# A gated mix of two long convolutions: four PSUM copies merged in pairs, and a hand-written order permuted

## The chip, the cores and the metric

The kernel runs on one core of one Trainium2 chip. The metric is device time in microseconds of one execution, as the median over several executions. The core's engines are named as the profile names them: PE (matrix multiply, with its weight loads shown as PEld), DVE (vector), ACT (scalar and activation functions), POOL (which here makes index tables and starts DMAs) and SP (which only starts DMAs). Each runs its own list of instructions in order; semaphores tie the lists together.

## The reference

Two sequence mixers work on the same input `x` of 2048 positions by 448 channels, and a gate of one value per position mixes their results. Each mixer is a causal convolution as long as the sequence, written as an FFT product. In A the convolution kernel `K` is itself computed, from 256 complex modes per channel; in B it is given.

```python
# A: u = x
dt = exp(log_dt)[:, None]; A = A_re + 1j*A_im; dB = dt*(B_re + 1j*B_im)
P = exp((dt*A)[:, :, None] * arange(2048))           # 448 x 256 x 2048
K = einsum("dn,dnl,dn->dl", C_re + 1j*C_im, P, dB).real
a = irfft(rfft(u, 4096) * rfft(K, 4096))[:2048] + u*Dskip
# B: q = x
k_shift = sum over t of k_pad[t : t+2048] * shift_k[:, 3-t]   # 4 taps
kv = k_shift * v
b = q * (irfft(rfft(kv, 4096) * rfft(ssm_k, 4096))[:2048] + kv*ssm_D)
# out
g = sigmoid((x * gate_w).sum(-1))
out = g*a + (1-g)*b
```

Inputs and output are bfloat16.

## The kernel before

**Work and tiling.** The 448 channels are cut into four groups `H` of 112 (28 columns in each of four partition blocks). For each group the kernel does three kinds of work, listed in `PLAN`: a table `T` (the sine and exponential tables of A's modes, their products, and from them K), a convolution of mixer B (`B`, `b`), and one of mixer A (`a`, for the last group `A`). For groups 0 to 2 a step `m` (`mix`, from line 1071) adds the two results and turns them to the output's layout; for the last group `end` (from line 980) does this in four quarters, `h` and `k` from 0 to 1.

A convolution is a Fourier transform written as matrix products in two levels: `spread` and `transform` go forward; `swapped` makes a copy with real and imaginary halves exchanged, by eight small DMAs; `products` multiplies the two spectra on DVE, two operations of 128 x 3584; `stage_a` and `stage_b` come back. After each block of matrix products the result is copied from PSUM to SBUF.

**Who copies.** The class `Sides` (line 346) gives each of some 400 such small steps to DVE or to ACT by one letter of the string `SIDES`: V is DVE, S is ACT. The same string decides for each of `swapped`'s DMAs whether POOL's queue (V) or SP's (S) starts it. Lines 355 to 390 hold the kinds of step: plain copy, add, scale and add, mask, negate.

**Order.** The program's 6,393 calls are not issued where they are written. `Order` (line 133) records them in a list, and `issue` (line 140) issues them in the order of the string `ORDER`, a permutation written out in runs of numbers. Each instruction is tied behind the one before it on its engine, so `ORDER` fixes every engine's list, DMA queues included. `SLOTS` and `ROOMS` (read in `slot` and `room`, lines 161 to 168) say which of eight SBUF buffers `q0` to `q7` and which of four PSUM rooms `ps0` to `ps3` each step uses. A room is two PSUM banks wide.

All instructions are issued from one line, so the profile shows L145 for all of them, and one tells them apart by tile and shape.

**Modes.** `Modes.run` (line 718) makes what the tables start from. For `A_re` and `A_im` it takes one room, with 448 values in each of its two banks (bank `f`), and copies it into three buffers: one holds group 0 (`hold`), one group 1, one groups 2 and 3. Every buffer is filled by two copies, one for each bank, so there are 2 x 3 x 2 = 12 copies. The groups' log-steps then feed `exps` and `levels`, which scale 224 columns at a time for the exponential and the sine.

**The start.** ACT's first step is to load the table of functions for the exponential; it then takes the exponential of `log_dt`, which a DMA brings. Sines need the other table, so ACT loads tables five times in the program.

**The end.** In `end`, each quarter does 33 matrix products (the sum over `G`), then on DVE a multiplication by the gate and an addition (`RK`), then 16 short matrix products (`relay`), then a negating copy (`q<-ps` 128x448), then four DMAs to the output, two on SP's queue and two on ACT's:

```python
evac.minus(laid(line(y0)[:, 0:4], H), pt[:, 0:448].rearrange(...))
for x in range(4):
    dmae[x % 2].dma_start(out_rows[x][:, y0:y0 + 4], lines[h][...])
```

In the built program the DMAs of SP and ACT take eight completion counters in turn, and a DMA that takes a counter again first waits, on the engine that starts it, until the earlier DMA of that counter has landed.

Of the kernel before, what the change touches and what calls it, by code (L numbers as in the profile page):

```python
# [24 lines left out]
NC = 112 // NQG  # L25
# [13 lines left out]
    "60254113451327565066707216435622473722641555230367571061240"  # L39
)  # L40
ROOMS = (
    "303201320132221133023000100332000020101102013331223132233010132231223133020313021221212111021000320232120101311331120231"
    "31230230312202203230211002013123100022133320222302200321202302202333012331301212103331312131332201202032310"
)
SIDES = (
    "SSSSVVSVVVVSVVSVVVVVVVVVSVVVSSVVVSSSSSVSVVSSVVSVVSVSSVVSVVVVVVVSSSSSSSSSSSSSSSSSVVVSVSSSVSSSSSSSSSSSSSSSSVSSSSVSVSSSSSSS"
    "SSSSSSSSSSSSSVSSVSSSSSSSSSSVSSSSSSSSSSSSSSSSSSVVSVSSSSSSSSSSSSSSSSSVVVVVVVVVSVVSVVVSSSSSSVSSSSSSSSSSSSVVSVSSSSSSSSSSVSVV"
    "SSSSSSSSSSSVSSSVVSSSSSSSSSSSVSSSSVVVVVVVVSVVVVSVVVSSSVSVVSSSSSSSSSSVVVSVVSSSSSSSSSSSSSSVSSSSSVSSSSSSVSSVSVSSVSSSSVSVVSSS"
    "VSSSSVSSVVVVSSSSSSSSSSVVVSSSSVSSSSVSSSVVSS"
)  # L50
ORDER = (
# [650 lines left out]
class Modes:  # L702
# [15 lines left out]
    def run(self):  # L718
        nc, V, evac = self.nc, self.nc.vector, self.evac
        for c, nm in enumerate(("A_re", "A_im")):  # L720
            pt = self.stepped(nm)
            for h0, h1, t in self.hold:
                for f in range(2):
                    evac(t[:, :, c].rearrange("p h (q w) -> p q h w", w=NC)[:, 4 * f:4 * f + 4],
                         pt[:, f, 0:448].rearrange("p (g h w) -> p g h w", g=4, w=NC)[:, :, h0:h1])
# [401 lines left out]
```

## Time and profile before

| | us |
|---|---|
| median of three executions | 249.13 (248.91 to 250.43) |
| the profiled execution, own time | 247.59 |
| its span, first to last instruction | 245.7 |
| granted TensorE clock, mean | 0.984 |

The profile gives for each engine the time in which it was busy, the idle time before an instruction together with what ended it, and groups of instructions of one shape with their mean duration. Durations of neighbours on an engine overlap a little, so a sum of durations is somewhat more than the busy time. A window shows the busy time of each engine in one stretch of the span. The chain of waits follows the last instruction back to whatever released it.

### The profile page before, as it was taken

The page shows a single profiled execution, that of the slowest core. Times are in us where ns is not written, and L with a number is a line of the kernel's source. Part 1 is how long each engine was busy: PE and PEld are TensorE (multiplying, and loading weights), DVE is VectorE, ACT ScalarE, POOL GpSimd, SP SyncE. Part 2 cuts the span into 40 slices and gives each one's busy share as a digit, 9 for nine tenths or more (in the row PEclk, how much of TensorE's full clock was granted, in tenths as well). Part 3 has the DMA queues.
Part 4 walks back from the last instruction along what each step waited for, and adds up shares of the span by engine and source line. Part 5 has one row for each costly group of instructions (what it writes and reads, how often), then busy time and mean ns, then how long its engine had stood idle before and what let it go on. Part 6 is the DMA issues. An engine that isn't in the chain of part 4 may idle for free.

```text
span 245.7 us, 12199 instructions
## 1 busy us (share of the span) xinstructions
PE 209.4 (85%) x5451; PEld 185.2 (75%) x5451; DVE 231.3 (94%) x399; ACT 219.0 (89%) x335; POOL 37.5 (15%) x109
## 2 busy tenths in 40 slices
PE   1557688888989999888999977999999999999970
PEld 1445256766979899788998866889999998998850
DVE  6999999999888999999999999999999999999980
ACT  3897999989999999999999999999999998657820
POOL 8600003040000014000002320000134220300000
PEclk9999799999999999999999999999999999999996
DMA  6999599999002189300476593000248720230046
GB/s 140 311 191 147 123 190 229 188 204 167 7 5 64 39 197 205 93 4 5 78 114 122 104 226 100 7 3 5 39 80 152 187 80 5 63 95 3 3 105 197
DMA packets 43443, 26.27 MB, mean 107 GB/s; under 512 B 34144, under 2 KB 40400, under 8 KB 43392
## 3 DMA queue, kind: packets, MB, share of 16 engines
q1 hardware_dynamic: 39088, 15.98, 30.6%
q0 software_dynamic: 3456, 8.60, 17.6%
q10 hardware_dynamic: 848, 0.92, 1.3%
q8 instruction: 42, 0.69, 1.1%
q14 instruction: 9, 0.07, 0.1%
HBM read 9.78 MB, written 2.87 MB: 51 GB/s over the span
## 4 chain that ended last, share of the span: by engine, by line
DVE 34%; ACT 32%; PE 21%; issue 6%; DMA 5%; DVEq 0%; ACTq 0%
PE ps L145 21%; ACT q L145 21%; DVE TQ L145 10%; DVE TP L145 9%; DVE q L145 6%; ACT G L145 4%; DVE natv L145 3%; DMA TP<-TP 2%; ACT ET L145 2%; ACT s_W L145 1%; DMA RK<-in_A_log_dt_dram 1%; DVE RK L145 1%; ACT RK L145 1%; DMA out_dram<-q 1%; DVE ET L145 1%
## 5 line engine op out<-in xcount | busy, mean ns | idle before, releaser
L145 ACT CAST q<-ps 128x896 bf16<-128x896 f32 (+3 forms) x168 | 131.6, 909 | 6.6 <-PE ps L145 6.4
L145 PEld LDWEIGHTS <-G 128*128 128x128 bf16 (+2 forms) x1136 | 35.5, 103 | 15.0 <-issue 6.0
L145 DVE TENSOR_TENSOR TQ<-TQ,ET 128x896 bf16<-128x896 bf16 (+2 forms) x70 | 45.9, 683 | 0.1
L145 PEld LDWEIGHTS <-q 128*128 128x128 bf16 (+2 forms) x784 | 41.0, 134 | 6.3 <-issue 3.5
L145 PE MATMUL ps<-q,s_W 128*128 128x112 bf16 (+1 forms) x544 | 32.6, 210 | 4.5 <-ACT q L145 2.3
L145 PE MATMUL ps<-TP,TQ 128*32 128x32 bf16 x1792 | 32.7, 240 | 2.8 <-DVE TQ L145 1.7
L145 PE MATMUL ps<-sa_R,q 128*128 128x128 bf16 x448 | 33.0, 229 | 1.5 <-issue 1.0
L145 DVE TENSOR_TENSOR q<-q,q 128x3584 bf16<-128x3584 bf16 (+1 forms) x22 | 32.3, 1510 | 1.2 <-ACT q L145 0.9
L145 PEld LDWEIGHTS <-s_W 128*128 128x128 bf16 x544 | 27.6, 97 | 7.6 <-issue 5.5
L145 PEld LDWEIGHTS <-TQ 128*32 128x32 bf16 x1792 | 29.6, 153 | 4.9 <-DVE TQ L145 1.9
L145 DVE TENSOR_TENSOR TP<-TP,ET 128x1792 bf16<-128x1792 bf16 (+3 forms) x25 | 31.7, 1270 | 0.6 <-DMA TP<-TP 0.5
L145 ACT ACTIVATE q<-hold 128x224 bf16<-128x224 f32 (+1 forms) x77 | 28.8, 461 | 0.4 <-DVE hold L145 0.3
L145 POOL DMA_DIRECT2D TP<-TP x15 | 13.4, 958 | 102.3 <-DVE TP L145 33.5
L145 POOL DMA_DIRECT2D q<-q x27 | 15.8, 638 | 57.5 <-DVE q L145 24.4
L145 PEld LDWEIGHTS <-natu 128*64 128x64 bf16 (+1 forms) x288 | 21.0, 208 | 4.6 <-DMA natu<-in_B_k_dram 3.1
L145 PE MATMUL ps<-q,G 128*128 128x56 bf16 (+1 forms) x640 | 20.3, 182 | 0.2 <-ACT q L145 0.2
L145 ACT ACTIVATE ET<-q 128x1344 bf16<-128x1344 int16 (+1 forms) x12 | 17.2, 1456 | 1.1 <-DVE TQ L145 1.0
L145 PE MATMUL ps<-Wc,natu 128*64 128x128 bf16 x224 | 16.0, 285 | 0.2 <-ACT q L145 0.2
L145 PE MATMUL ps<-Wc,natv 128*64 128x128 bf16 x224 | 15.2, 283 | 0.4
L145 PEld LDWEIGHTS <-natv 128*64 128x64 bf16 x224 | 14.7, 212 | 1.1 <-issue 0.2
L145 DVE TENSOR_TENSOR TQ<-TQ 128x448 bf16<-128x448 bf16 (+2 forms) x35 | 15.3, 443 | 0.1
L145 PE MATMUL ps<-G 112*32 112x336 bf16 (+3 forms) x448 | 13.8, 274 | 1.3 <-DVE natv L145 1.1
(97 smaller groups left out, 289.6 us busy)
## 6 DMA issues: line engine op xcount, KB each, us to landing
q<-q SPq DMA_DIRECT2D x37, 112.0 KB, 3.7
TP<-TP POOLq DMA_DIRECT2D x9, 448.0 KB, 5.8
q<-q POOLq DMA_DIRECT2D x27, 112.0 KB, 3.9
natu<-in_B_k_dram SPq DMA_DIRECT2D x2, 896.0 KB, 7.2
natv<-in_B_v_dram SPq DMA_DIRECT2D x8, 224.0 KB, 4.7
q<-in_B_ssm_k_dram SPq DMA_DIRECT2D x16, 112.0 KB, 3.9
natu<-in_A_u_dram SPq DMA_DIRECT2D x8, 224.0 KB, 5.8
TP<-TP POOLq DMA_DIRECT2D x6, 224.0 KB, 4.0
```

What stands on the lines that cost most here:

```text
L145: ins = f(*args, **kw)
```

## The change

Two things change, one small in code and one large in data.

In `Modes.run` a buffer that holds a single group is filled by one copy that reads both banks of the room (224 columns), instead of two copies of 112. The buffer of groups 2 and 3 keeps its two copies. Twelve copies become eight, and the program has 6,389 calls.

```diff
             for h0, h1, t in self.hold:
+                src = pt[:, :, 0:448].rearrange("p f (g h w) -> p f g h w", g=4, w=NC)
+                if h1 - h0 == 1:
+                    evac(t[:, 0, c].rearrange("p (f g w) -> p f g w", f=2, w=NC), src[:, :, :, h0])
+                    continue
                 for f in range(2):
-                    evac(t[:, :, c].rearrange("p h (q w) -> p q h w", w=NC)[:, 4 * f:4 * f + 4],
-                         pt[:, f, 0:448].rearrange("p (g h w) -> p g h w", g=4, w=NC)[:, :, h0:h1])
+                    evac(t[:, :, c].rearrange("p h (q w) -> p q h w", w=NC)[:, 4 * f:4 * f + 4], src[:, f, :, h0:h1])
```

All four strings are new: `ORDER`, `SIDES`, `SLOTS`, `ROOMS`. `PLAN` and every other function are as before. Read out per engine, the two programs differ like this:

- Besides the merged copies, 30 steps go from DVE to ACT and 20 from ACT to DVE. DVE has 384 instructions instead of 399, ACT 347 instead of 335, counting its table loads.
- ACT loads tables six times instead of five: a first sine, on 64 columns, now stands ahead of the exponential of `log_dt`, with its own table load.
- Eight more of the small DMAs of `swapped` go to POOL's queue: POOL starts 50 DMAs instead of 42, SP 92 instead of 100.
- The merged copies for `A_re` and `A_im` run on ACT but for one; six of the twelve were on DVE.
- In `end`, the last three quarters' relays stand one behind the other after the last sum over `G`. Before, each relay stood between two sums, and only two stood after the last one. Twelve of the sixteen output DMAs now stand behind the last three negating copies.
- Nearly every step is moved by some places within its engine's list; the sequence of the large stages is the same.

```diff
 SIDES = (
-    "SSSSVVSVVVVSVVSSVVVVVVVVVSVVVSSVVVSSSSSVSVVSSVVSVVSVSSVVSVVVVVVVSSSSSSSSSSSSSSSSSVVVSVSSSVSSSSSSSSSSSSSSSSVSSSSVSVSSSSSSS"
...
+    "SSSSVVSVVVVSVVSSVVVVVVVVSVSSSSSSVVVSSVSSVVSVVSSSVVSSSVVVSVVSSSSSSSSSSSSSSSVSVVSVVSSSVSSVSVSSSSSSSSSSSVSSSSSSSSSSSSSSSSSS"
...
```

More of the change, by code (lines that the diff above doesn't have):

```diff
@@ L38 @@
 SLOTS = (
-    "60254113451327565066707216435622473722641555230367571061240"
+    "20403116354647120522757642301265663671204711735354460250172"
 )
 ROOMS = (
-    "303201320132221133023000100332000020101102013331223132233010132231223133020313021221212111021000320232120101311331120231"
-    "31230230312202203230211002013123100022133320222302200321202302202333012331301212103331312131332201202032310"
+    "012131000231110120223323211032233303311333021332202103210131202001330010101103330222033213220320321121111121101303200031"
+    "01021032232203032203303301000222002203212132020330103132102322310010331331023320213332130130121201010013332"
 )
 SIDES = (
[L46 to L49, printed above, removed]
+    "SSSSVVSVVVVSVVSSVVVVVVVVSVSSSSSSVVVSSVSSVVSVVSSSVVSSSVVVSVVSSSSSSSSSSSSSSSVSVVSVVSSSVSSVSVSSSSSSSSSSSVSSSSSSSSSSSSSSSSSS"
+    "SSSSSSSSSSSSSVSSSSSSSSSSSSSSSSSSSSSSSSSVSVVVVVVSSSSSSSSSSSSSSSSSVVVVVSVVVVVSVVVSSSSSSVSSSSSSSSSVVVVVVSSSSSSSSSVSVSVSSSSS"
+    "SSSSSSVVVVSVSSSSSSVSSSSSSVSSVSVVVSVVVVSVVVSVVVSSSSSSSSSSSSSSSSVSVVVSVVSSSVSSSSVSSVVSSSSSSSSSSSVSSSVSSSSSSSSSSVSVSVSSSVSS"
+    "VSSSVSSSVSSSSSSSSSVVSSSSSVSVSSSSSSVSSS"
 )
 ORDER = (
[60 rows of a table removed]
[59 rows of a table added]
 )
```

119 rows, old and new, of the table ORDER are left out of this document.

## The prediction

> **What bounds the kernel now.** I read the busy times first, then windows of the span.
>
> ```profile
> PE 209.4 (85%) x5451; PEld 185.2 (75%) x5451; DVE 231.3 (94%) x399; ACT 219.0 (89%) x335; POOL 37.5 (15%) x109
> 0.00:203.10 203.10, 174.78 (x4478) 154.77 (x4478) 196.56 (x354) 194.59 (x296) 35.42 (x105) 0.99 0.56 115
> 0.00:212.00 212.00, 183.36 (x4770) 162.79 (x4771) 205.43 (x359) 201.31 (x307) 35.42 (x105) 0.99 0.54 110
> 212.00:237.50 25.50, 25.21 (x653) 21.93 (x650) 24.22 (x38) 17.10 (x28) 2.05 (x4) 1.00 0.17 44
> ```
>
> The first row is from the page. The others are windows: length, then busy time (and instructions) of PE, PEld, DVE, ACT, POOL, then granted clock and DMA share. DVE and ACT are both nearly full, and full at the same time. Up to 203.1 us ACT idles 203.1 - 194.6 = 8.5 us; up to 212.0 us DVE idles 212.0 - 205.4 = 6.6 us. So no single engine's saving comes straight off the span there: what one engine saves only counts if the other keeps up. After 212 us that is different. DVE is busy 24.2 of 25.5 us, ACT only 17.1, and PE's records fill 25.2, of which weight loads need 21.9. The tail is bound by DVE and perhaps PE, with ACT having 8 us to spare.
>
> What happens at 212 us is seen in the timeline (start, length, engine, operation, count, idle time before it):
>
> ```profile
> 208.03 3.96 DVE L145 TENSOR_TENSOR q<-q,q 128x3584 bf16<-128x3584 bf16 x2
> 236.56 0.95 PE L145 MATMUL ps<-q,G 128*128 128x28 bf16 x32
> ```
>
> The first is the last pair of wide products, for mixer A's third group; behind it come the last stages of three convolutions. The second is the last sum over G; it ends at 237.5 us, 8.2 us ahead of the span's end.
>
> **The steps that change sides.** Counted net by shape: DVE loses five mode copies, eight scalings of 224 columns or less, three negating copies of 448, one copy each of 1024 and 768 columns and one mask of 2048; it gains two copies of 512 and two of 896. ACT gains one mode copy, the eight scalings, the three negations, the 1024, the 768, the mask and a table load, and loses two 512 and two 896. What else moves cancels. The rows that price this (busy time, mean ns of one):
>
> ```profile
> L145 DVE COPY hold<-ps 128x112 f32<-128x112 f32 x3 | 0.8, 270 | 0.0
> L145 DVE TENSOR_SCALAR q<-hold 128x224 int32<-128x224 f32 x26 | 6.6, 299 | 0.0
> L145 DVE TENSOR_SCALAR q<-ps 128x448 bf16<-128x448 f32 x7 | 4.2, 618 | 0.7 <-PE ps L145 0.6 <-ACT q L145 0.2
> L145 DVE CAST q<-ps 128x512 bf16<-128x512 f32 x9 | 5.9, 685 | 0.1
> L145 DVE CAST q<-ps 128x896 bf16<-128x896 f32 x2 | 2.2, 1088 | 0.8 <-issue 0.8
> L145 DVE CAST q<-ps 128x1024 bf16<-128x1024 f32 x2 | 2.4, 1220 | 0.6 <-PE ps L145 0.6
> L145 DVE CAST q<-ps 128x768 bf16<-128x768 f32 x1 | 1.0, 953 | 0.0
> L145 DVE TENSOR_SCALAR G<-q,mask 128x2048 bf16<-128x2048 bf16 x5 | 3.6, 747 | 0.0
> L145 ACT COPY q<-ps 128x224 f32<-128x224 f32 x4 | 1.3, 336 | 1.5 <-DVE q L145 1.5
> L145 ACT ACTIVATE q<-hold 128x224 int32<-128x224 f32 x13 | 4.9, 421 | 0.0
> L145 ACT ACTIVATE q<-ps 128x448 bf16<-128x448 f32 x9 | 4.5, 546 | 5.7 <-DMA out_dram<-q 4.1 <-PE ps L145 1.6
> L145 ACT CAST q<-ps 128x512 bf16<-128x512 f32 x43 | 26.4, 637 | 3.3 <-PE ps L145 3.1
> L145 ACT COPY TQ<-ps 128x896 f32<-128x896 f32 x1 | 0.9, 897 | 0.0
> L145 ACT CAST q<-ps 128x896 bf16<-128x896 f32 x62 | 56.9, 1028 | 0.9 <-PE ps L145 0.9
> L145 ACT CAST q<-ps 128x1024 bf16<-128x1024 f32 x50 | 52.4, 1103 | 0.2 <-PE ps L145 0.2
> L145 ACT CAST q<-ps 128x768 bf16<-128x768 f32 x3 | 2.4, 812 | 1.4 <-PE ps L145 1.4
> L145 ACT ACT_TABLE_LOAD x5 | 6.4, 1283 | 1.3 <-PEq L1111 1.2
> L145 ACT ACTIVATE G<-q,mask 128x2048 bf16<-128x2048 bf16 x3 | 6.3, 2101 | 0.0
> ```
>
> The merged copy reads 224 columns from two banks; no row shows that. On ACT I take 0.34 us, the copy of the same width from one bank. On DVE it lies between one and two of the 0.27 us copies; I take 0.34 again. Six DVE copies become one: -1.62 + 0.34 = -1.28 us.
>
> *DVE:* -1.28 - 8 x 0.299 - 3 x 0.618 + 2 x 0.685 + 2 x 1.088 - 1.22 - 0.95 - 0.75 = -4.9 us of durations. *ACT:* the mode copies were four of 224 and two of 112 and become seven of 224, between 0.34 and 1.0 us more, taken as 0.5; then + 8 x 0.421 + 3 x 0.546 - 2 x 0.637 - 2 x 0.897 (the two 896 that leave are copies to TQ) + 1.10 + 0.81 + 2.10 + 1.28 = +7.7 us.
>
> Durations overlap, so fewer instructions also means fewer overlaps:
>
> ```profile
> 234.55 1.15 DVE L145 TENSOR_SCALAR q<-ps 128x448 bf16<-128x448 f32 x2
> 234.71 1.42 ACT L145 ACTIVATE q<-ps 128x448 bf16<-128x448 f32 x3 [1.35 <-PE ps L145]
> ```
>
> Two of 0.618 take 1.15 us and three of 0.546 take 1.42: about 0.09 us of overlap each on DVE, 0.11 on ACT. With 15 instructions fewer and 12 more, DVE's busy time falls by 3.5 us (4.9 if no overlap is lost) and ACT's grows by 6.4 (7.7).
>
> **Where it falls.** Walking down the new DVE list to the last wide pair, with the same prices: the merged copies (-1.28), seven scalings net (-2.09), the mask (-0.75) and a 112-wide scaling, priced like the others (-0.30), against one copy of 512 (+0.69) and three of 896 net (+3.26). That is -0.5 us with ten instructions fewer, so nothing, within 0.5 us either way. All of DVE's saving, about 4 us, lies behind the wide pair, in the tail that DVE bounds.
>
> ACT is the reverse. Up to its last copy of the transform that feeds that pair, it has +0.5 for the modes, eight scalings net (+3.4), the mask (+2.1), the table load (+1.3), three copies of 896 fewer net (-2.8), and four copies of 896 that stood behind it and are now ahead (+4.1): +8.5 us, less 1.3 for overlap, about +7. In the old order ACT's part of that transform was about done at 203.1 us, with 194.6 us of work behind it. Now it is 201.6 us of work. With the old 8.5 us of idle time it would end at 210.1, and the pair, which started at 208.0, would be 2.1 us late. So what counts is how much idle time the extra work fills. The first filler, in the timeline and the row of that sine:
>
> ```profile
> 1.20 1.28 ACT L145 ACT_TABLE_LOAD   x1 [1.20 <-PEq L1111]
> 4.22 0.21 ACT L145 ACTIVATE TP<-RK 112x4 bf16<-112x4 bf16 x1 [1.74 <-DMA RK<-in_A_log_dt_dram]
> L145 ACT ACTIVATE TP<-TP 128x64 bf16<-128x64 int16 x2 | 0.5, 264 | 0.0
> ```
>
> ACT waits 1.74 us for log_dt's DMA. The sine that moves there (0.26 us) and the second table load (1.28) go into that hole and cost the span at most 0.3 us, unless DVE makes the sine's input late; then up to 1.3. That leaves the pair 2.1 - 1.5 = 0.6 us late. Against it stands a stall that I expect to go:
>
> ```profile
> L145 DVE TENSOR_TENSOR TP<-TP,ET 128x3584 bf16<-128x3584 bf16 x9 | 18.1, 2016 | 0.5 <-DMA TP<-TP 0.5
> 129.78 5.62 DMA TP<-TP
> ```
>
> DVE waits 0.5 us for an accumulating DMA on TP, which takes 5.6 us in the chain of waits. The new order puts about 8 us of DVE work between that DMA's start and its user. I put the end of the wide pair at 212.0 us, unchanged, within 0.6.
>
> The Trainium skill, page "ScalarE: Activation LUTs", section "Table sets: the hidden batching unit", says to batch calls by table set since every switch costs a load, which speaks against the sixth load. The trace agrees on its length, 1283 ns; if it lay on the path, the forecast below would be 1.3 us higher, 249.1.
>
> **DMA queues.** The eight swaps that go to POOL stand behind POOL's accumulating DMAs, and one of the last table's accumulating DMAs now stands behind two of them, which wait for ACT's copies. From the page's list of DMA issues, and median time to landing:
>
> ```profile
> q<-q SPq DMA_DIRECT2D x37, 112.0 KB, 3.7
> q<-q POOLq DMA_DIRECT2D x27, 112.0 KB, 3.9
> ```
>
> So a moved swap lands 0.2 us later, which I count at nothing: the user of that accumulating DMA, the back half of the table, stands some 20 us of DVE work behind its source. If that cover is gone, DVE waits the difference, under 2 us.
>
> The Trainium skill, page "SBUF — State Buffer", section "SBUF: two separate sides", warns that a DMA started from POOL can be held up while DVE runs certain operations. With DVE at 94% the trace shows only those 0.2 us, so I give that rule no weight.
>
> **The tail.** DVE has 4 us less to do between 212.0 and 237.5 us. PE can give up nothing if its recorded 25.2 us is its floor, and 3.6 us if the 21.9 us of weight loads is. ACT has 8 us of room and gets about as much work as it had after the pair. I take the middle, 2.0 us: the last sum ends at 235.5.
>
> Then the output DMAs:
>
> ```profile
> 237.67 0.38 PE L145 MATMUL ps<-RK,minus 128*32 128x112 bf16 x16 [0.15 <-DVE RK L145]
> DMA to landing us min/median/max: 1.9/2.9/3.2
> 238.83 3.44 SPq L145 DMA_DIRECT2D out_dram<-q  x5
> 240.24 0.54 ACT L145 ACTIVATE q<-ps 128x448 bf16<-128x448 f32 x1 [4.12 <-DMA out_dram<-q]
> 240.81 0.86 ACTq L145 DMA_DIRECT2D out_dram<-q  x2
> 241.72 0.55 SPq L145 DMA_DIRECT2D out_dram<-q  x1
> ```
>
> The first row is a relay in the timeline, the second the output DMAs' time to landing, the others are the timeline again. The last DMA starts at 241.72, 2.9 us after the one at 238.83 whose counter it takes: it waited for that landing. From its start to the span's end are 3.9 us. In the new order three relays (0.4 us each) and ACT's two negating copies (0.54) follow the last sum, so ACT's copies are done 1.5 us behind it. ACT then starts DMAs 0.4 us apart, and the last DMA takes the counter of the second of these: started at 1.9, landed at 4.8 to 5.1, its successor started then and the span over 3.9 later, 8.8 to 9.0 us behind the last sum instead of 8.2. Without that reuse the twelve, six a queue and 0.4 apart from 1.0 on, would be out by 3.4 and the span over at 7.3. So the end costs between -0.9 and +0.8 us; I take +0.7, since the waits are in the program.
>
> **Sum.** The profiled execution took 247.59 us: span 245.7 and 1.9 outside, which stays. It becomes 247.6 + 0 - 2.0 + 0.7 = 246.3. That execution lies 1.5 us below the median of 249.13, so the forecast of the median is 249.1 - 1.3 = 247.8 us.
>
> **Rivals.** *Full gain:* PE gives up 3.6 us and the DMAs' end costs nothing: 249.1 - 3.6 = 245.5. For it: DVE's 4 us lie just where DVE is 95% busy. Against it: PE's records are full there. *ACT becomes the bound:* nothing of its other idle time is filled, the hole at the start included, so the wide pair is 2.1 us late; PE gives up nothing and the DMAs cost 0.7: 249.1 + 2.8 = 251.9. It decides from about 6.5 us of ACT idle time ahead of the pair: above that every microsecond goes to the span. For it: ACT is at 194.6 of 203.1 us already. Against it: the hole is plain. *The permutation shifts idle time only:* PE's records are its floor and the merge saves nothing that counts, so the change does not do what it says; with the DMAs, 249.1 + 0.7 = 249.8.
>
> **Numbers.** Forecast 0.43, full gain 0.25, ACT bound 0.18, shift only 0.14. The range from 245.4 to 251.2 takes in all but the ACT rival and the ends of the others. About 1% (2.5 us) is what a measurement of this kernel can tell from no change. Under 246.6 lie most of the full gain (0.22) and the low edge of the forecast (0.06): 0.28. Above 251.6 lies most of the ACT rival: 0.15. Within 1%: 0.57.
>
> **What would show it.** In the new profile: DVE busy near 227.5 us and ACT near 225; the log_dt wait on ACT nearly gone, filled by the second table load; the last 3584-wide pair ending at 212 within 0.6 (213.5 or later speaks for the ACT rival); the last sum over G ending near 235.5; ACT's busy time behind the pair above 85%; and a last output DMA that starts about 3 us behind the last copy. The forecast falls if the pair moves by more than 1.5 us either way, or if DVE idles over 3 us in the tail for PE.

## The result, and the profile after

The changed kernel takes 250.41 us (median of 20 executions, 248.86 to 252.49) against 249.24 for the kernel before beside it (20 executions). The ratio is 1.0047, 95% interval 1.0025 to 1.0068: about 1.2 us slower. Run again beside some of the experiments (e5 below) it was 1.0027 (0.9998 to 1.0055). The forecast was a gain of 1.3 us.

Its page, busy time of each engine (compare the first row of the prediction):

```profile
PE 209.8 (85%) x5451; PEld 185.1 (75%) x5451; DVE 228.2 (92%) x384; ACT 224.1 (90%) x347; POOL 42.1 (17%) x117
```

DVE lost 3.1 us and ACT gained 5.1, about as forecast. Windows, cut at the end of the last wide pair and at the end of the last sum over G:

```profile
0.00:212.08 212.08, 182.91 (x4699) 161.74 (x4701) 205.62 (x349) 201.91 (x309) 42.05 (x117) 0.96 0.57 115
212.08:238.30 26.22, 25.99 (x727) 22.81 (x723) 20.88 (x33) 21.25 (x36) 0.00 (x0) 1.00 0.03 6
```

The pair ends at 212.08 us, against 211.99 in the profile of the kernel before. Behind it the tail did not shrink: 26.2 us instead of 25.5. DVE now idles 5.3 us there, and PE is busy for 25.99 of 26.22. From the last sum to the span's end are 9.5 us instead of 8.1. So between these two profiles the loss lies behind the pair: 0.7 us in the tail and 1.3 in the end. That is more than the 1.2 us of the medians, because the profiled execution of the kernel before lies 1.5 us below its median and that of the changed kernel 0.5 below; groups of profiles further down correct for it.

The start, in the timeline of ACT: the new sine and both table loads stand where ACT waited for log_dt.

```profile
1.19 1.28 ACT L144 ACT_TABLE_LOAD   x1 [1.19 <-PEq L1113]
3.14 0.26 ACT L144 ACTIVATE TP<-TP 128x64 bf16<-128x64 int16 x1 [0.66 <-DVE TP L144]
3.41 1.28 ACT L144 ACT_TABLE_LOAD   x1
4.71 0.21 ACT L144 ACTIVATE TP<-RK 112x4 bf16<-112x4 bf16 x1
```

Around the pair, the timeline shows a wait that was not there before: ACT stands still for 4.8 us until DVE's second wide product has ended.

```profile
210.06 2.02 DVE L144 TENSOR_TENSOR q<-q,q 128x3584 bf16<-128x3584 bf16 x1
212.19 1.56 ACT L144 CAST q<-ps 128x512 bf16<-128x512 f32 x3 [4.81 <-DVE q L144]
```

The copy is the first of mixer B's last group into the buffers `pair` that two convolutions share. The new `SLOTS` puts the second half of `pair` into q6, which holds the spectrum `K` that the wide products still read. Before, it went into q7, and ACT copied from about 208 us on.

### The profile page after: what moved, and what is told of

It reads as the page before. It is cut to its first block, busy times and chain, and to the rows that moved or that the text cites. A ratio compares the mean times of both kernels' runs of the same rounds, so it can differ in the third digit from the quotient of the medians.

```text
span 247.8 us, 12203 instructions
## 1 busy us (share of the span) xinstructions
PE 209.8 (85%) x5451; PEld 185.1 (75%) x5451; DVE 228.2 (92%) x384; ACT 224.1 (90%) x347; POOL 42.1 (17%) x117
## 4 chain that ended last, share of the span: by engine, by line
ACT 42%; PE 22%; DVE 12%; issue 8%; SPq 4%; DMA 4%; ACTq 0%; DVEq 0%
ACT q L144 33%; PE ps L144 22%; SPq L144 4%; DVE TQ L144 3%; ACT ET L144 3%; DMA q<-in_B_ssm_k_dram 3%; DVE q L144 3%; DVE TP L144 2%; DVE natv L144 2%; ACT RK L144 2%; ACT L144 2%; ACT natv L144 1%; DVE RK L144 1%; DMA q<-q 1%; DVE G L144 1%
## 5 line engine op out<-in xcount | busy, mean ns | idle before, releaser
L144 ACT CAST q<-ps 128x896 bf16<-128x896 f32 (+4 forms) x167 | 131.1, 935 | 9.5 <-DVE q L144 5.1
L144 PEld LDWEIGHTS <-q 128*128 128x128 bf16 (+2 forms) x784 | 42.5, 137 | 13.5 <-issue 6.1
L144 PEld LDWEIGHTS <-G 128*128 128x128 bf16 (+2 forms) x1136 | 34.3, 102 | 12.9 <-issue 4.7
L144 PE MATMUL ps<-q,s_W 128*128 128x112 bf16 (+1 forms) x544 | 33.9, 211 | 3.6 <-ACT q L144 3.2
L144 PE MATMUL ps<-sa_R,q 128*128 128x128 bf16 x448 | 34.5, 230 | 1.8 <-DVE q L144 0.8
L144 PE MATMUL ps<-TP,TQ 128*32 128x32 bf16 x1792 | 33.7, 240 | 2.4 <-issue 1.5
L144 ACT ACTIVATE q<-hold 128x224 bf16<-128x224 f32 (+1 forms) x83 | 30.6, 468 | 0.1
L144 POOL DMA_DIRECT2D q<-q x35 | 19.2, 594 | 44.3 <-PE ps L144 24.6
L144 DVE CAST q<-ps 128x512 bf16<-128x512 f32 (+3 forms) x17 | 12.8, 757 | 4.2 <-ACT q L144 2.5
L144 PE MATMUL ps<-Wc,q 128*64 128x128 bf16 x224 | 10.0, 238 | 6.7 <-DVE q L144 3.4
```

Of the source, the lines that this page charges most:

```text
L144: ins = f(*args, **kw)
```

## The experiments

All ratios are to the kernel before, run beside each. "Tail" is from the end of the wide pair to the end of the last sum over G, "end" from there to the end of the span, both from the one profiled execution.

| kernel | tail, us | end, us | ratio (95%) |
|---|---|---|---|
| before | 25.5 | 8.1 | 1 |
| e3, before, merge alone | 25.6 | 8.6 | 0.9983 (0.9957 to 1.0008) |
| e7, before, pair held | 26.6 | 9.0 | 1.0039 (1.0013 to 1.0065) |
| e9, before, less DVE work | 25.6 | 8.9 | 1.0020 (0.9992 to 1.0048) |
| e10, before, less PE work | 25.6 | 8.5 | 1.0001 (0.9966 to 1.0036) |
| e11, before, merge and another end | 25.5 | 7.9 | 0.9997 (0.9970 to 1.0023) |
| e13, before, stacked end | 25.2 | 9.9 | 1.0010 (0.9979 to 1.0041) |
| e14, before, less DVE and PE work | 24.8 | 8.4 | 0.9976 (0.9946 to 1.0006) |
| changed | 26.2 | 9.5 | 1.0047 (1.0025 to 1.0068) |
| e5, changed again | 26.0 | 9.6 | 1.0027 (0.9998 to 1.0055) |
| e6, changed, pair moved | 26.1 | 9.3 | 1.0030 (0.9999 to 1.0060) |
| e12, changed, late sine | 26.4 | 9.7 | 1.0046 (1.0018 to 1.0073) |
| e15, e6 and copies to ACT | 27.5 | 9.3 | 1.0045 (1.0017 to 1.0074) |
| e4, changed, end put back | 26.8 | 7.6 | 0.9984 (0.9955 to 1.0014) |
| e8, e6 and e4 | 26.7 | 8.4 | 1.0006 (0.9981 to 1.0031) |
| e16, e15 and e4 | 27.8 | 8.2 | 1.0000 (0.9966 to 1.0034) |
| e17, changed, DMA order put back | 26.3 | 8.9 | 1.0028 (1.0001 to 1.0054) |
| e18, changed, relay order put back | 27.2 | 8.5 | 1.0030 (1.0003 to 1.0058) |

One interval is about 0.3% either way, 0.7 us, so single rows settle little; what settles is the groups. Tail and end come from one profile each.

> The changed kernel itself, as the yardstick for the three beside it on the same chip: ratio to before 1.003 to 1.007, ACT's idle time of 4.8 us ahead of 212.2 us, the last sum over G ending near 238.3 and the span 9.4 us behind it.

**The merge alone (e3).** The changed `Modes.run` in the kernel before, with the engines that the change gives the merged copies.

> The kernel before with the merged mode copies alone (eight instead of twelve, on the engines that the changed kernel gives them), order and all other sides as before. Theory: the copies lie ahead of the first table where neither engine is at its limit for long; DVE's busy time falls by 1.6 us, ACT's rises by about 0.5 us, ratio to before 0.998 to 1.001. Rival 'the merged copy is dear' (it reads two banks or stands where a log-step waits for it): a copy of 0.6 us or more, or the sines of the first group later by over 0.5 us, ratio above 1.002.

The groups of e3 that hold them, on ACT and on DVE:

```profile
L145 ACT COPY hold<-ps 128x224 f32<-128x224 f32 x2 | 0.7, 334 | 1.5 <-PE ps L145 1.5
```

```profile
L145 DVE COPY q<-ps 128x224 f32<-128x224 f32 x1 | 0.4, 391 | 0.1
```

On ACT, both banks in one copy cost what 224 columns of one bank cost (336 ns in the prediction's row). No difference in the time can be measured: the code change is not the cause.

**The held buffer (e1, e2, then e6, e7).** Two letters of `SLOTS` exchanged, in the changed kernel (e1) and the other way round in the kernel before (e2):

```diff
-    "...54460250172"
+    "...54470250162"
```

> The changed kernel with two letters of SLOTS exchanged: the second half of the last two-convolution pair goes to q7, the swapped copy of mixer A's last group to q6. Theory 'buffer': ACT's 4.81 us of idle time ahead of 212.19 us (it waits for DVE's second wide product, which reads q6) goes, ACT copies the first stage of convolution B's group 3 from about 208 us on, as before the change; the tail behind the wide pair gets 1.5 to 2.5 us shorter and the median falls from 250.4 to 248-249. Rival 'PE floor': the 25 us of matrix products behind the pair set the tail anyway; ACT's wait goes but the last sum over G stays within 0.5 us of 238.3 and the median within 0.5 us of 250.4. Rival 'swap': the eight small DMAs of the swapped copy now wait for the wide pair and delay the last products; then the last K product is later than 228.3 us and nothing is gained.

> The kernel before with the opposite exchange: the second half of that pair goes to q4, which the last wide product still reads, the swapped copy to q7. Nothing else changes. Theory 'buffer': ACT idles about 3.5 to 5 us until the second wide product has ended near 212 us, and the kernel gets 1.5 to 2.5 us slower: ratio to before 1.006 to 1.010. Rival 'PE floor' or 'the order sets the tail': ratio 0.999 to 1.002, the wait appears in the trace but the last sum over G does not move from 237.5 by more than 0.5 us.

Both missed their question. Which step reads a buffer's old content is fixed by `ORDER`, and the exchange let another step write first: in e1 the swapped copy's small DMAs, in e2 ACT's copies into the pair. A wide product then read other values, after waiting for them (2.8 us in e1, ratio 1.0197, 1.0148 to 1.0246; 0.5 us in e2, ratio 1.0003, 0.9974 to 1.0033). e6 and e7 move the places in the list as well; no engine's own list changes but the DMA queues' in e6:

```diff
 # e6, ORDER, behind the second wide product
- 6025 ... 6026 ... 6027 ... 6024 6023 6021 ... 6022 ... 6028 ... 5483-5498 5652 4927-4990
+ 5483-5498 5652 6025-6027 6024 6023 6021-6022 6028 4927-4990
```

> e2 done properly: the kernel before with the pair's second half in the buffer that the wide products still read (q4), the swapped copy in q7, and the list positions such that the copies into the pair come behind the product that reads q4; no engine's own list changes. Theory 'buffer': ACT idles 3.5 to 5 us until DVE's second wide product ends near 212 us; the last sum over G ends 0.8 to 2 us later than 237.5; ratio to before 1.003 to 1.008. Rival 'the tail has room': the wait appears, the last sum moves by under 0.4 us and the ratio is 0.999 to 1.002.

> e1 done properly: pair's second half in q7, swapped copy of mixer A's last group in q6, and the eight small DMAs of that copy issued behind the second wide product instead of ahead of it (in e1 they overwrote the spectrum that the product was still to read, so the product read other values and waited for them). Theory 'buffer': ACT's idle time ahead of 212 us falls from 4.8 us to under 1.5, its first copy into the pair starts at 208-209 us, the last sum over G ends at 236.0 to 237.2 instead of 238.3, ratio to the changed kernel 0.991 to 0.996. Rival 'PE floor': ACT's wait goes, but the last sum stays at 238.3 within 0.4 and the ratio to the changed kernel is 0.998 to 1.002. Rival 'swap': the later small DMAs hold up the last products, the wait moves to DVE at about 219-225 us, no gain or up to 1 us lost.

In the kernel before, the held buffer costs what was expected. ACT's row in e7's timeline, then PE's window around the pair in e7 and in the kernel before:

```profile
213.21 1.84 ACT L145 CAST q<-ps 128x256 bf16<-128x256 f32 x4 [3.07 <-DVE q L145]
```

```profile
206.00:215.00 9.00, 7.98 (x239) 7.51 (x237) 8.97 (x7) 4.87 (x10) 2.05 (x4) 1.00 0.44 106
```

```profile
206.00:215.00 9.00, 8.86 (x308) 8.29 (x305) 8.96 (x8) 6.20 (x11) 2.05 (x4) 1.00 0.21 47
```

ACT does not empty PSUM and PE idles more: by 0.9 us in these windows, and by 0.5 if e7's window is moved by the 1.1 us by which its pair ends later (207.13 to 216.13 us, PE busy 8.38). The tail is 1.1 us longer: PE never makes it up. In the changed kernel, taking the buffer out of the way brought nothing: the tail is 26.1 us and the ratio 1.0030, beside 1.0027 for e5. e6's timeline shows why:

```profile
211.67 1.07 ACT L145 CAST q<-ps 128x512 bf16<-128x512 f32 x2 [2.71 <-DVE q L145]
214.20 0.58 ACT L145 CAST q<-ps 128x512 bf16<-128x512 f32 x1 [1.46 <-DVE q L145]
```

Each stage's result is copied twice from one PSUM room, once to each half of the pair, and the second copy waits for the first. Where `SIDES` gives the first one to DVE, it stands behind a wide product there. So one wait took the place of another.

**What bounds the tail (e9, e10, e14, e15).** e9 shrinks three additions of DVE behind the pair, e14 also leaves 28 products of PE out, e10 shrinks eight:

```diff
 # e9, e14: mix
-        V.tensor_tensor(out=o, in0=o, in1=x, op=ALU.add)
+        V.tensor_tensor(out=o[:, 0:1], in0=o[:, 0:1], in1=x[:, 0:1], op=ALU.add)
 # e14: the last group of conv_A
-            stage_a(nc, places, R, whole(U, evac), (X, S), [...])
+            stage_a(nc, places, R, whole(U, evac), (X,), [...])
```

> The kernel before with the three additions of mix shrunk to their first 28 of 1792 columns (the mixed sum of groups 0 to 2 then lacks mixer A's part but for one position in 64): DVE has about 2.9 us less to do behind the last wide pair, in the tail that the prediction took to be bound by DVE; every order and buffer is as before. Theory 'PE floor' (matrix products fill the core from about 157 us on, PE idle under 2 us up to the last sum over G): the last sum ends within 0.5 us of where it was (25.5 us behind the pair), DVE idles 2.5 to 3 us more, ratio to before 0.997 to 1.001. Rival 'DVE bound', the prediction's step: the last sum 1.5 to 3 us earlier, ratio 0.988 to 0.994.

> The kernel before with the eight products over minus in the last pair's second stage shrunk from 224 to 28 columns (the last pair's result then lacks the subtracted term at seven of eight positions): PE has some 1.2 to 1.7 us less to do at 222 to 227 us, nothing else changes. Theory 'PE floor': the last sum over G ends 1.0 to 1.7 us earlier (23.8 to 24.5 us behind the pair instead of 25.5), ratio to before 0.993 to 0.997. Rival 'DVE bound': the last sum within 0.4 us, PE idles the 1.2 to 1.7 us more, ratio 0.998 to 1.001.

> e9 with fewer matrix products as well: the first inverse stage of mixer A's last group leaves out its second term (28 of 56 products of 128 columns at 226.5 to 230.6 us of the kernel before; the last group's A part is then wrong by that term), and DVE's three additions are shrunk as in e9. Theory 'PE floor': PE has about 2.0 us less to do, the last sum over G ends 1.0 to 2.0 us closer to the wide pair than in e9 (23.6 to 24.6 us behind it against 25.6), ratio to before 0.992 to 0.997. Rival 'ACT or the chain of waits': ACT's four wide copies of that stage (3.6 us) or DVE's products set the pace; the last sum within 0.5 us of e9's, ratio 0.999 to 1.002.

Windows from the pair's end to the last sum's end, first e9, then e14:

```profile
212.99:238.63 25.64, 25.50 (x656) 22.17 (x653) 21.64 (x38) 17.26 (x28) 2.05 (x4) 1.00 0.17 44
```

```profile
212.73:237.57 24.84, 23.83 (x625) 20.50 (x624) 21.76 (x39) 17.14 (x28) 2.05 (x4) 1.00 0.17 45
```

With 2.6 us less to do, DVE idles 4.0 us instead of 1.3, and the tail is as long as before. PE is busy 25.50 of 25.64. With some 1.7 us of PE's work gone as well, the tail gets 0.8 us shorter, and the rest turns into waits of PE for DVE, in e14's timeline:

```profile
228.32 0.67 PE L145 MATMUL ps<-sa_R,q 128*128 128x128 bf16 x8 [0.47 <-DVE natu L145]
229.38 1.05 PE L145 MATMUL ps<-sa_R,q 128*128 128x128 bf16 x14 [0.40 <-DVE natu L145]
```

In e10 the last sum did not move, as its rival said, but the test was too small to decide: the products of 28 columns instead of 224 still take 0.17 us instead of 0.26, PE is busy only 0.3 us less in the tail (24.9 against 25.2) where 1.2 to 1.7 were meant, and it gave that back at waits. The shrunk product and the longest of these waits:

```profile
226.81 0.17 PE L145 MATMUL ps<-natv,minus 128*128 128x28 bf16 x1
227.32 0.57 PE L145 MATMUL ps<-q,G 128*128 128x56 bf16 x16 [0.34 <-DVE natu L145]
```

e15 gives DVE's three copies of the shared stage to ACT, in e6:

```diff
 # e15, ORDER; three letters of SIDES V -> S
- 5463 5483-5498 5652 4927-4990 5499 5464 4991-5054 5481 5500 5482
+ 5481-5482 5463-5464 5483-5498 5652 6025-... 4927-4990 5499-5500 4991-5054
```

> e6 (the changed kernel with the pair's second half in q7) and DVE's three copies of convolution B's first stage (512 columns) given to ACT, all six at ACT's idle time ahead of the wide pair's end. Theory 'copies': ACT copies from 207 to 211 us where it idled 4.8 us, the wide pair ends 0.7 us earlier, DVE has 2 us less; the last sum over G ends 25.0 to 25.7 us behind the wide pair's end (26.2 in the changed kernel), ratio to the changed kernel 0.993 to 0.998. Rival 'PE floor': PE's idle time stays 0.3 to 0.5 us around the pair and the last sum moves by under 0.4 us: ratio to the changed kernel 0.998 to 1.002.

The pair ended 0.5 us earlier, and nothing came of it. DVE's timeline and the window behind the pair, in e15:

```profile
217.33 0.69 DVE L145 CAST q<-ps 128x512 bf16<-128x512 f32 x1 [3.73 <-ACT q L145]
```

```profile
211.59:239.05 27.46, 26.38 (x731) 23.07 (x731) 19.61 (x31) 20.40 (x34) 1.54 (x3) 1.00 0.15 39
```

DVE idles 3.7 us in one piece and the last sum is not earlier. So in the tail PE's list takes most of the time: time freed on DVE or ACT brought nothing, and work taken from PE brought half of itself (0.8 of 1.7 us in e14). It is not PE's list alone, since in e15 PE idles for 1.1 us of the tail and waits for no engine that the profile names.

**The end (e4, e8, e11, e13, e16, e17, e18).** e4 puts the relays back between the sums and each copy's four DMAs behind it; e17 does only the DMAs, e18 only the relays:

```diff
 # e4, ORDER, the last calls of end (quarter 0: sum 6165-6197, relay 6200-6215, DMAs 6217-6220; the next quarters 56 calls later each)
- 6165-6197 ... 6368-6383 6198 6274-6275 6312-6327 6384 6199 6328 6387 6200-6215 6332 6385 6216 6330 6329 6386 6388 6217 6219-6220 6218 6331
+ 6368-6383 6165-6197 ... 6274-6275 6384 6312-6327 6385-6388 6198 6328 6199 6329-6332 6200-6220
```

> The changed kernel with the order of the end alone put back in kind: the relays stand between the sums over G, each negating copy and its four DMAs right behind its relay. Theory 'end': the span ends 8.0 to 8.6 us behind the last sum over G instead of 9.4, the median falls by 0.8 to 1.4 us to 249.0-249.6; the pair's end at 212 and ACT's 4.8 us wait stay. Rival 'last copy': the last relay still waits for the last sum's gating and the last DMAs' landing sets the end, so the span ends 9.2 us or more behind the last sum and the median stays within 0.4 us of 250.4.

> The changed kernel with the relays stacked behind the last sum over G as they are there, and only the order of the output DMAs put back: each copy's four DMAs right behind it, quarter 3 first, then 2, then 0. Theory 'DMA order': the span ends 8.2 to 8.8 us behind the last sum over G instead of 9.5, with the last sum where it was; ratio to before 0.998 to 1.001, as with e4. Rival 'relays': the copies come late, so the DMAs do whatever their order; 9.2 us or more, ratio 1.003 to 1.005.

> The changed kernel with quarter 3's relay moved between the sums as in e4, and the output DMAs in the changed kernel's order behind the last copies. Theory 'DMA order': still 8.8 us or more behind a last sum over G that is about 0.6 us later (in e4 the relay waits there for ACT's copy of its PSUM room); ratio 1.003 to 1.005. Rival 'relays': as e4, 7.6 to 8.2 us and ratio 0.998 to 1.001.

> The kernel before with the last three quarters' relays stacked behind the last sum over G and their twelve DMAs behind the last copies, as in the changed kernel; quarters, rooms and sides as before. Theory 'end': the span ends 9.0 to 9.6 us behind the last sum over G instead of 8.1 and the last sum comes 0 to 0.4 us earlier (PE no longer does relays ahead of it); ratio to before 1.002 to 1.006, which would be most of what the changed kernel lost. Rival 'no loss at the end': ratio 0.998 to 1.001 and the span ends within 8.5 us of the last sum.

ACT's DMAs at the end, in the timelines of the changed kernel and of e4:

```profile
237.35 0.95 PE L144 MATMUL ps<-q,G 128*128 128x28 bf16 x32
239.67 4.13 ACTq L144 DMA_DIRECT2D out_dram<-q  x6
```

```profile
238.46 0.96 PE L144 MATMUL ps<-q,G 128*128 128x28 bf16 x32
238.97 0.85 ACTq L144 DMA_DIRECT2D out_dram<-q  x2
240.49 2.54 ACTq L144 DMA_DIRECT2D out_dram<-q  x4
```

In the changed kernel six DMAs stand on ACT's queue from 1.4 us behind the last sum on and take 4.1 us to start. In e4 two of them start 0.4 us ahead of the last sum's end, and the four others, from 1.1 us behind it on, take 2.5. The end is 1.8 us shorter; 0.6 of it is given back, because quarter 3's relay then waits for ACT's copy out of its room ahead of the last sum:

```profile
237.95 0.38 PE L144 MATMUL ps<-RK,minus 128*32 128x112 bf16 x16 [0.43 <-ACT q L144]
```

> e6 and the end order of e4 together. If both causes are separate they add: the last sum over G at 237 to 238 (in e4 the interleaved relays delayed it to 239.4 of a span of 247.0), the span 7.6 to 8.2 us behind it, ratio to the changed kernel 0.988 to 0.993, to before 0.992 to 0.998. If the end order takes back what the buffer gives, it is no faster than the faster of e4 and e6.

> e15 with the end of e4: if the end is worth 1.4 us in the changed kernel and the copies something more, ratio to before 0.993 to 0.998, faster than both; if only the end counts, as e4: 0.997 to 1.000.

e8 is no faster than e4, so moving the buffer adds nothing. The three kernels with e4's end (e4, e8, e16) have ratios of 0.9984, 1.0006 and 1.0000; the five with the change's end untouched (changed, e5, e6, e12, e15) 1.0047, 1.0027, 1.0030, 1.0046 and 1.0045. e4 differs from the changed kernel, e8 from e6 and e16 from e15 in nothing but the end, and each time the old end is faster. The means differ by 0.4%, 1.0 us, which is the whole loss. e17 and e18 stay at 1.003, so neither half is enough by itself, as far as such intervals tell. In the kernel before, the same stacking made the end 9.9 us in the profile, but the ratio of 1.0010 leaves open whether it costs anything there.

e11 was to beat both: e3, and in the kernel before the last sum's gating ahead of the negating copy of quarter 0 and no DMA left for last.

> A version meant to beat both: the kernel before with the merged copies of e3 and another order of the end: the last sum's gating and addition go ahead of the negating copy of quarter 0 on DVE, and the DMA of quarter 1 that stood last goes to its quarter. Theory 'end': the last negating copy is done 1.1 us earlier and no DMA is left behind the others, so the span ends 7.0 to 7.5 us behind the last sum over G instead of 8.1; with the merge the ratio to before is 0.993 to 0.997. Rival: the DMAs' landing sets the end, 8 us behind as before; ratio 0.997 to 1.000, as in e3.

It did not. The last copy is done 2.1 us behind the last sum instead of 3.3, but the span still ends 7.9 us behind it. None of these kernels beats the kernel before by more than its interval.

**The early sine (e12).** Calls 179 and 180 moved behind the next sines; ACT loads five tables.

> The changed kernel with the first sine (and the multiplication that uses it) moved back to the next sine of its kind, so that ACT loads tables five times again. Theory 'free': the sine and its load lay in the wait for log_dt, which comes back (1.2 to 1.8 us) with the exponential of log_dt at 4.2 us instead of 4.7; the later milestones move by under 0.5 us, ratio to the changed kernel 0.998 to 1.001, to before 1.001 to 1.005. Rival 'dear': the sixth load and the half microsecond by which log_dt's exponential is late are paid in full: ratio to the changed kernel 0.993 to 0.997.

```profile
4.00 0.20 ACT L145 ACTIVATE TP<-RK 112x4 bf16<-112x4 bf16 x1 [1.52 <-DMA RK<-in_A_log_dt_dram]
6.26 0.35 ACT L145 COPY hold<-ps 128x224 f32<-128x224 f32 x1 [1.15 <-PE ps L145]
```

The wait for log_dt is back and the first mode copy is 0.4 us earlier than in the changed kernel (6.68), but the wide pair ends at 212.22 and the ratio is the same: the sixth load is free here. The Trainium skill, page "ScalarE: Activation LUTs", section "What ACT_TABLE_LOAD costs", adds a drain of about 1.4 us to each load; in the changed kernel the next operation starts at 4.71, 0.02 us behind the end of the load that began at 3.41, so the trace shows no such drain.

## Why the prediction was wrong

**The step that failed: the tail.** "I take the middle, 2.0 us: the last sum ends at 235.5." It ended at 238.3, and the tail is 0.5 to 0.9 us longer than before in every profile with this order (26.0 to 26.4 against 25.5). The prediction had named the floor, PE's recorded 25.2 of 25.5 us, and then chosen a value halfway to the 21.9 us of weight loads. e9 shows that halfway was not there: 2.6 us less on DVE gave nothing. The view that pointed to it was the chain of waits, which the prediction did not use for this stage. Its longest steps from the wide pair to the last sum, in the kernel before and in the changed one (start, length, what):

```profile
208.03 3.96 DVE q L145 x2
211.99 2.00 DVE natv L145 x2
214.65 12.17 PE ps L145 x305
226.96 9.17 PE ps L145 x210
```

```profile
201.62 3.88 DVE q L144 x2
205.86 5.69 PE ps L144 x164
211.86 14.82 PE ps L144 x416
227.13 10.20 PE ps L144 x244
```

From 214.65 us to 236.1 us the chain runs through PE alone. A DVE that is 95% busy beside it has no share in that length. In the changed kernel the chain goes over to PE already at 205.9, and PE has more left at the pair's end: 727 products in 25.99 us against 653 in 25.21. What is moved behind the pair are sums of the last table:

```profile
211.86 1.65 PE L144 MATMUL ps<-TP,TQ 128*32 128x32 bf16 x92 [0.31 <-issue]
```

```profile
210.10 1.69 PE L145 MATMUL ps<-TP,TQ 128*32 128x32 bf16 x96
```

That these 0.8 us of work make the longer tail is read from the windows; no run put them back, and an earlier pair may be part of it (below). ACT's 4.8 us of idle time is the conspicuous wait in the profile after, and it is not the cause here (e6, e15), though it costs 1 us in the kernel before (e7). The prediction let ACT get "about as much work as it had after the pair". Up to the pair ACT's work came out as counted (201.9 us by 207.4 us, 201.6 forecast), but it then stood still, and 21.3 us are left behind the pair against 17.1 before.

The rule by which the prediction took weight loads as PE's other bound is in the Trainium skill too: page "Perfetto Trace Analysis", section "Identifying the Most-Contended Engine", says that the busy share of matrix products is a poor measure of how near PE is to its limit, and to use that of weight loads, beside the rate of arithmetic. Here weight loads fill 22.81 of 26.22 us, 87%, and products 99%; that 2.6 us less for DVE brought nothing (e9) and 1.7 us less for PE brought 0.8 (e14) agrees with the 99%.

**The end: right mechanism, somewhat small.** Forecast 8.8 to 9.0 us behind the last sum; it is 9.3 to 9.7 in five profiles with that end (mean 9.5), against 8.1 to 9.0 (mean 8.6) in six with the old one (before, e3, e7, e9, e10, e14). The old end of 8.1 was the shortest of its six. The difference of the means, 0.9 us, is about the 0.7 of the sum; that it is worth 1.0 us of time is what e4, e8 and e16 show. The parts differ from the forecast both ways: in the changed profile the last DMA, which takes the counter of one started 2.8 us earlier, starts 4.6 us behind the last sum (forecast 4.8 to 5.1), but from its start to the span's end are 4.9 us, where the sum took the 3.9 of the kernel before.

**The shares of busy time: right.** DVE at 228.2 (227.5 forecast), ACT at 224.1 (225). The merged copy takes 0.33 us on ACT and 0.39 on DVE (0.34 forecast for both).

**Up to the pair: as forecast in this profile, somewhat better by groups.** It ends at 212.08 (212.0 within 0.6), and the log_dt wait is filled and worth nothing (e12). But the profile of the kernel before is a weak yardstick, being a short execution. In five more profiles with its order up to there (e7, e9, e10, e13, e14) the pair ends at 212.7 to 213.8 us, and in six more with the changed order (e4, e5, e8, e12, e17, e18) at 211.6 to 212.6. The means, 213.0 and 212.2 with the two profiles above, say that the new order gained some 0.8 us ahead of the pair. The tail, 0.7 us longer, took that back, so that the last sum is no later than with the old order (238.3 to 238.6 in changed, e5, e12 and e17; 237.5 to 239.5 in before, e9 and e10), and the end's 0.9 us are left. This fits with the end alone giving back the whole loss. It is read from one profile of each kernel, and no run tested it. The stall for the accumulating DMA on TP, 0.5 us, is gone: that group now shows 0.0 idle time. The swaps on POOL's queue now land in 4.1 us against 3.7 on SP's. The chain of waits has one step of 2.0 us on such a DMA, just ahead of 201.6 us, that the kernel before has not; the pair is not later for it.

**The rivals.** Nearest is the one that got the least chance, 0.14: PE's records are the floor and the DMAs cost 0.7 us, 249.8 us. With the tail's 0.7 us on top it would have said 250.5. That 250.4 us lies inside the stated range is owed to the range's width, which took in this rival, and not to the forecast's mechanism. ACT behind the pair was 81% busy, not over 85; and the sign that was to fell the forecast, DVE idle for over 3 us in the tail, is there with 5.3.

## What to carry to other kernels

Before a saving is counted, follow the chain of waits through the very stage in which it lies: an engine at 95% beside a chain that ran through another one yielded nothing here, and its freed time turned into idle time. Between two bounds for a stage, test which one holds by shrinking one engine's work there, rather than taking the middle. When an order, an assignment of engines and of buffers are permuted together, look at what stands behind the last computation: here a few relays and output DMAs at the end decided the sign. And compare profiles in groups: among six with the same order up to the wide pair, the pair's end differed by 1.8 us.

## What the runs showed of the hardware

The granted TensorE clock dips early in both profiles, further in the changed kernel's. Below, the clock row of the kernel before, then of the changed one (40 slices of 6.1 and 6.2 us, in tenths):

```profile
PEclk9999799999999999999999999999999999999996
```

```profile
PEclk9976689998899999999999999999999999999995
```

It goes down to 0.6 at 19 to 31 us of the changed kernel, where DVE and ACT are full and PE is not; the wide product that ends at 106.8 us in the kernel before ends at 107.1, dips and new order together. From the pair to the last sum the windows show 1.00 for both kernels, so the clock has no part in the length of the tail. And the same end, built the same way, varied by 0.9 us between profiles (8.1 to 9.0 us), as much as the difference that the prediction worked out from single DMA starts.
